# Attention feeding a feed-forward layer: the inverse sums laid out by partition in DRAM, filler products allowed earlier, and a new set of plan shifts

## The chip, the cores and the metric

The kernel runs on one core of one Trainium2 chip. The metric is device time in microseconds (us). Three runs of the kernel before gave 2834.0, 2835.68 and 2836.08 us, a median of 2835.68 us.

## What is computed

The reference is an attention over pooled keys, followed by a feed-forward layer on its result:

```
kv_flat = mean over 4x4 windows of kv, reshaped to [4, 768, 128] @ w_sr
s = q @ kv_flat^T / sqrt(128);  s -= max(s);  a = exp(s);  a /= a.sum() + 1e-9
x = a @ kv_flat                          # 4 batches x 12288 tokens x 128
h = x @ w_in;  g = h - tanh(h);  out = g @ w_out        # w_in 128 x 2048, w_out 2048 x 128
```

The weights are given in double precision and the inputs in single precision. The kernel forms the products in half precision with a high and a low part of each operand. For small `h` it computes `h - tanh(h)` from `h * tanh(c h)^2`.

## The kernel before, in words

**Tiling.** 49152 tokens are cut into 96 groups of 512, 24 to a batch. A group has four tiles of 128 tokens. For each tile PE (TensorE) makes scores against the 768 keys (L737, six products of 384 columns, tile `s`). DVE (VectorE) takes the maximum (`nm`, L745), ACT (ScalarE) the exponential and its row sum (`e`, L751) and a half precision copy (`a`, L756), and POOL (GpSimd) the low part (L760). The DMA queue of SP then transposes `a` into `at` (L764), one transpose for a tile, so that keys lie on the partitions. When four tiles of a group are there, 18 products of 512 columns form `x` (L814).

**The division.** The row sums of a group lie as [128 partitions, 4 tiles]. `inverse` (L778, L779) sums and inverts them into `inv`. The division (L827) needs these 512 numbers as one row, token by token, on every partition. So SP stores `inv` to a DRAM tile `sums_row` (L782) and reads it back, broadcast to all 128 partitions, as `row` (L786). Groups 0 and 1 do without DRAM: there PE makes the row with products against an identity, and ACT copies it (L796). DVE's `divide` then gives `xf`, from which `x2`, the high and the low part of the input of the feed-forward, is made.

**The feed-forward.** A group has eight units of 256 hidden columns. A unit is six products of 512 columns into `h` (L854 to L856), tanh and square on ACT (`t`, L882, L885), `gg` on DVE (L888), its high part `gh` on POOL or, for one unit of eight, on ACT, its low part `gl` on DVE (L899), and six products into `acc` (L860 to L862). There are two buffers of `h` and of `gg`, and one of `acc` and of `x`.

**Keys.** The keys of batches 1 to 3 are loaded in 12 pieces each (`kc`, 512 KB, L536) and pooled by DVE in 48 reductions of one size (`kvp`, L540), while the groups before run. The keys of batch 0 are pooled by PE at the start: it multiplies each of the 16 places of a window by `w_sr` and sums them in `s` (L551).

**What sets the order.** Everything above is first entered as steps of a `Plan` with an engine, an estimated duration and a place. `run` (L146) then schedules the list by these estimates; the tables `SHIFT` and `FIRST` move the place of every step of one kind (`FIRST` for the first 28 places), and `EARLY` moves a whole group. The order that comes out is the program order of each engine. Engines wait for each other by semaphores only. SP issues its DMAs in that order too, and a DMA that has to wait holds all behind it. While `run` schedules, it looks for pauses on PE in the first 75 us of its own estimate: where one is longer than 1 us, `busy` (L1143) puts products there that nobody reads (`spare`, L1151). Before, this begins only after the last pooling step of batch 0, which bears the name `pooled`.

Of the kernel before, what the change touches and what calls it, by code (L numbers as in the profile page):

```python
# [9 lines left out]
F32 = mybir.dt.float32  # L10
# [6 lines left out]
ALU = mybir.AluOpType  # L17
# [4 lines left out]
P = 128  # L22
# [45 lines left out]
class Plan:  # L68
# [8 lines left out]

    SHIFT = {
        "divide": 0.1, "exps": -1.11, "forth": 0.58, "fro": 3.81, "g_high": 1.19, "g_low": 0.61,
        "inverse": 0.91, "largest_score": -1.19, "largest_x": -0.1, "load_row": 1.46,  # L80
        "pool": 12.74, "q_high": 0.33, "q_low": 0.21, "result": -0.72, "scores": -0.17,
        "square": -0.48, "store": -1.33, "store_row": 2.86, "store_x": -1.51, "tanh": 0.29,
        "turn_weights": 0.78, "values": 1.09, "weight_high": 2.59, "weight_low": 0.56,
        "x_high": 1.25, "x_low": -6.78,
    }

    FIRST = {
        "add": -1.15, "copy": -0.44, "copy_row": -2.77, "diagonals": 1.67, "divide": 2.2,
        "exps": -0.64, "forth": 2.94, "fro": 5.42, "g_high": 7.15, "high": 1.2, "inverse": -0.87,
        "keys_wide": -2.2, "largest": 1.37, "largest_score": -0.82, "largest_share": 0.12,  # L90
        "largest_x": 0.26, "load_q": -1.09, "load_row": 1.54, "load_words": 1.25, "low": -1.78,
        "lower": 1.13, "pool": 13.24, "q_high": -1.56, "q_low": 1.38, "result": -1.78,
        "rows": 2.23, "scaled": -1.29, "scores": -3.23, "scores_wide": -2.15, "shares": -0.67,
        "shift": 1.11, "size": 0.26, "sizes": 3.78, "small": 3.11, "square": -0.1, "store": 0.64,
        "store_row": 4.53, "store_x": 3.1, "sum_of_rows": -0.86, "sums": 5.55, "tanh": -0.84,
        "times": -0.33, "top": -0.25, "turn_weights": 1.58, "upper": -1.52, "values": 0.12,
        "values_high": 0.24, "weight_high": 0.13, "weight_low": 1.91, "within": 0.68,
        "x_high": -1.77, "x_low": -4.87,
    }
    UNTIL = 28  # L100
    SOON_FIRST, FIRST_US = 0.111, 150.0

    EARLY = {"attention 0": 2.1, "attention 1": 6.6, "attention 2": 8.5, "attention 3": 2.2, "weights_in": 2.9, "weights_out": 18.9}
    KEEP_US = 75.0
    SOON = 0.153
    TURN = 0.19
# [39 lines left out]
    def run(self, between):  # L146


        n = len(self.ops)
# [16 lines left out]
            for k in need[i] | behind[i]:  # L166
                then[k].append(i)
        free, ready, done, begun, order, was_wide = {}, {}, [0.0] * n, [0.0] * n, [], True
        pooled = False
        for i in range(n):  # L170
            if not left[i]:
                ready.setdefault(self.ops[i][1], []).append((0.0, i))
        while any(ready.values()):
            best = None
            for e, q in ready.items():
                if q:
                    starts = []
                    for r, i in q:
                        held = free.get("port", 0.0) if self.ops[i][5] else 0.0
                        starts.append((max(free.get(e, 0.0), r, held), self.ops[i][0], i, r))  # L180
                    first = min(starts)[0]
                    soon = first + (self.SOON_FIRST if first < self.FIRST_US else self.SOON)
                    step, i, start, r = min((p, i, t, r) for t, p, i, r in starts if t <= soon)
                    if best is None or (start, step, i) < best[:3]:
                        best = start, step, i, e, r
            now, _, i, e, r = best
            ready[e].remove((r, i))
            step, _, us, _, late, port, dma, wide, dram = self.ops[i]
            if e == "PE":
                us += self.TURN if wide and not was_wide else 0.0  # L190
                was_wide = wide
                pause = now - free.get(e, 0.0)
                if pooled and pause > 1.0 and now < self.KEEP_US:
                    order.append((free[e], -round((pause - 0.6) / 0.3)))
                pooled = pooled or self.names["pooled"] == i
            free[e] = now + us
            if dma:
                landed = free.get("rows", 0.0) if dram == "read" else 0.0
                free["dma"] = max(free.get("dma", 0.0), now + us, landed) + dma
                if dram == "rows":  # L200
                    free["rows"] = now + us + late
                late += free["dma"] - (now + us)
            if port:
                free["port"] = now + us
            begun[i], done[i] = now, now + us + late
            order.append((now, i))
            for k in then[i]:
                left[k] -= 1
                if not left[k]:
                    f = self.ops[k][1]  # L210
                    r = [done[j] + (self.HOP if self.ops[j][1] != f else 0.0) for j in need[k]]
                    r = max(r + [begun[j] + 0.01 for j in behind[k]])
                    ready.setdefault(f, []).append((r, k))
# [3 lines left out]
        held, at = None, 1 + next(k for k, (_, i) in enumerate(order) if i == self.names["known"])  # L217
# [18 lines left out]
def attention_then_ffn(ctx: ExitStack, tc: tile.TileContext, q, kv, w_sr, w_in, w_out, out):  # L236
# [7 lines left out]
    V, A, PL, PE, SP = nc.vector, nc.scalar, nc.gpsimd, nc.tensor, nc.sync  # L244

    B, C, N = q.shape
    K, W = kv.shape[2], kv.shape[3]
# [5 lines left out]
    NGT = B * NG  # L253
# [35 lines left out]
    sums_all = const.tile([P, 2, TT, 2], F32, name="sums_all")  # L289
    ident = const.tile([P, P], F32, name="ident")  # L290
    xs = dram.tile([C, 2, B * N], F16, name="xs")
    sums_row = dram.tile([NGT, TT, P], F32, name="sums_row")

    plan.tile("ident", "ident", 1, lambda: None)
    def identity(step):
# [233 lines left out]
    def keys(b, s0):  # L529
# [25 lines left out]
        if b:  # L555
            gap, cut = 6, 4
            sb(kvp, "kvp", [P, K], F32, 1)
            for j in range(K // KB):
                s, key = s0 - gap * (K // KB - j), f"kc.{b}.{j}"
                sb(key, "kc", [P, KB, W], F32, 5)  # L560
                plan.op(s - 6, "SP", 0.5, partial(load, j, KB, key), (), (key,), late=2.0, dma=1.3,
                        dram="read", after=("unit", *divmod(int(s) - 8, UN)))
                for k in range(cut):
                    plan.op(s + k * gap / cut, "DVE", 0.33, partial(pool, j, KB, k, key), (key,),
                            ((kvp, (j, k)),))
        else:

            tags = [("t", 2), ("gg", 2), ("kc", 5)] * 2 + [("kc", 5)] * 3
            tags += [(("gh", 4), ("gl", 4))] * 4 + [("kc", 5)] * 3
            for n, tag in enumerate(tags):  # L570
                s = s0 - 40 + n
                if isinstance(tag[0], tuple):
                    for c, (name, bufs) in enumerate(tag):
                        key = f"kc.{b}.{n}.{c}"
                        sb(key, name, [P, KH], F32, bufs)
                        plan.op(s + c / 2, "SP", 0.45, partial(load_places, n, c, key), (), (key,),
                                late=2.0, dma=0.5)
                        plan.op(s + c / 2, "PE", 0.72, partial(product_of_place, n, (c,), (key,)),
                                (key,), ((pk, c),), wide=True)
                else:  # L580
                    key = f"kc.{b}.{n}"
                    sb(key, tag[0], [P, K], F32, tag[1])
                    plan.op(s, "SP", 0.45, partial(load_places, n, None, key), (), (key,), late=2.0,
                            dma=1.0)
                    plan.op(s, "PE", 1.44, partial(product_of_place, n, (0, 1), (key, key)), (key,),
                            (pk,), name="pooled" if n == W - 1 else None, wide=True)

        sb(vs, "vs", [P, 2], F32, 2)
        sb(vt, "vt", [P, 2, K], F16, 2)
# [94 lines left out]
    def attention(g, s0):  # L684
# [94 lines left out]
            V.reciprocal(out=plan[inv], in_=plan[inv])  # L779

        def store_row():
            SP.dma_start(out=sums_row[g].rearrange("t p -> p t"), in_=plan[inv])  # L782

        def load_row():
            r = sums_row[g : g + 1].rearrange("g t p -> g (t p)")
            SP.dma_start(out=plan[row], in_=r.to_broadcast([P, G]))  # L786


        def sum_of_rows():
            for t in range(TT):  # L790
                by = plan[inv][:, t : t + 1].to_broadcast([P, P])
                PE.matmul(out=plan[f"row_at.{g}"][:, t * P : (t + 1) * P], lhsT=by, rhs=ident,
                          start=True, stop=True)

        def copy_row():
            A.copy(out=plan[row], in_=plan[f"row_at.{g}"])  # L796

        s1 = s0 + 2 * TT
        plan.op(s1, "DVE", 0.25, inverse, (sums, "ident"), (inv,), late=0.1)
# [2 lines left out]
            plan.op(s1, "PE", 1.3, sum_of_rows, (inv, "ident"), (row_at,), late=0.2, wide=True)  # L802
            plan.op(s1, "ACT", 0.51, copy_row, (row_at,), (row,), late=0.1)
        else:
            plan.op(s1, "SP", 0.5, store_row, (inv,), (f"dram.{g}",), late=10.0, dma=0.8,
                    dram="rows")
            plan.op(s1, "SP", 0.5, load_row, (f"dram.{g}",), (row,), late=3.2, dma=0.65,
                    dram="read")
# [15 lines left out]
        plan.tile(f"most_x.{g}", f"most_x.{g}", 1, lambda: None)  # L824

        def divide():
            V.scalar_tensor_tensor(out=plan[xf], in0=plan[x], scalar=plan[vs][:, 0:1],  # L827
                                   in1=plan[row], op0=ALU.mult, op1=ALU.mult)

        def x_high():  # L830
            A.copy(out=plan[x2][:, 0], in_=plan[xf])
# [178 lines left out]
    def attention_any(b):  # L1010
# [31 lines left out]
        with tc.For_i(0, N, G) as place:  # L1042
# [18 lines left out]
                SP.dma_start(out=at[:, :, tok], in_=a.rearrange("p a k -> p (a k)"), transpose=True)  # L1061
            V.tensor_scalar(out=inv, in0=inv, scalar1=1e-9 * 2.0**LIFT, scalar2=None, op0=ALU.add)
            V.reciprocal(out=inv, in_=inv)
            SP.dma_start(out=sums_row[0].rearrange("t p -> p t"), in_=inv)
            row = t("row", [P, G])
            r = sums_row[0:1].rearrange("g t p -> g (t p)")
            SP.dma_start(out=row, in_=r.to_broadcast([P, G]))
            x = ps.tile([P, G], F32, tag="x", name="x_any", bufs=1)
            for n in range(KT):
                for k, (l, r) in enumerate(((n, n), (KT + n, n), (n, KT + n))):  # L1070
                    PE.matmul(out=x, lhsT=vv[:, l], rhs=at[:, r], start=(n == 0 and k == 0),
                              stop=(n == KT - 1 and k == 2))
            xf, x2 = t("xf", [P, G]), t("x2", [P, 2, G], F16, 3)
            V.scalar_tensor_tensor(out=xf, in0=x, scalar=by_batch[:, b, 6:7], in1=row,
                                   op0=ALU.mult, op1=ALU.mult)
            A.copy(out=x2[:, 0], in_=xf)
            V.tensor_tensor(out=x2[:, 1], in0=xf, in1=x2[:, 0], op=ALU.subtract)
            SP.dma_start(out=xs[:, :, bass.ds(place + b * N, G)], in_=x2)
# [129 lines left out]
```

## Time and profile before

| | |
|---|---|
| median of three runs | 2835.68 us (2834.0 to 2836.08) |
| profiled execution | 2835.5 us, span 2833.8 us |
| granted TensorE clock, mean | 0.997 |
| PE busy | 2795.2 us, 99% |
| DVE busy | 2682.0 us, 95% |
| ACT busy | 2596.9 us, 92% |
| POOL busy | 1346.5 us, 48% |

A busy share is an engine's time in instructions over the span; register, branch and DMA-issuing instructions are not counted in it. A row of the timeline gives the start, the time busy, the engine with the line and the names (out, arrow, in), and in brackets the idle time before it with what ended it. The granted clock is the share of full speed that the chip allowed TensorE.

### The profile page before, as it was taken

The page shows a single profiled execution, that of the slowest core. Times are in us where ns is not written, and L with a number is a line of the kernel's source. Part 1 is how long each engine was busy: PE and PEld are TensorE (multiplying, and loading weights), DVE is VectorE, ACT ScalarE, POOL GpSimd, SP SyncE. Part 2 cuts the span into 40 slices and gives each one's busy share as a digit, 9 for nine tenths or more (in the row PEclk, how much of TensorE's full clock was granted, in tenths as well). Part 3 has the DMA queues.
Part 4 walks back from the last instruction along what each step waited for, and adds up shares of the span by engine and source line. Part 5 has one row for each costly group of instructions (what it writes and reads, how often), then busy time and mean ns, then how long its engine had stood idle before and what let it go on. Part 6 is the DMA issues. An engine that isn't in the chain of part 4 may idle for free.

```text
span 2833.8 us, 39602 instructions
## 1 busy us (share of the span) xinstructions
PE 2795.2 (99%) x13430; PEld 1320.9 (47%) x13430; DVE 2682.0 (95%) x3201; ACT 2596.9 (92%) x3311; POOL 1346.5 (48%) x1057
## 2 busy tenths in 40 slices
PE   7999999999999999999999999999999999999998
PEld 4444444444444444444444444444444444444443
DVE  8899999999999999999999999999999999999997
ACT  7899999989999999998999999999999999999986
POOL 1455444444445454445445454444444544545442
PEclk9999999999999999999999999999999999999999
DMA  8544456555454446654544444566554444444440
GB/s 235 88 94 92 95 113 110 119 107 102 87 101 86 101 86 120 119 116 104 89 97 88 98 86 108 108 122 117 104 90 91 96 88 98 86 99 88 90 79 28
DMA packets 736421, 285.03 MB, mean 101 GB/s; under 512 B 665168, under 2 KB 692944, under 8 KB 736208
## 3 DMA queue, kind: packets, MB, share of 16 engines
q1 hardware_dynamic: 736208, 282.41, 50.0%
q8 instruction: 107, 1.75, 0.3%
q14 instruction: 106, 0.87, 0.2%
HBM read 79.23 MB, written 50.52 MB: 46 GB/s over the span
## 4 chain that ended last, share of the span: by engine, by line
PE 57%; DVE 26%; ACT 8%; issue 6%; DMA 1%; POOL 0%; DVEq 0%; SPq 0%; ACTq 0%; POOLq 0%
DVE gl L899 10%; PE s L737 8%; DVE gg L888 8%; PE x L814 7%; PE h L854 7%; PE h L856 7%; PE h L855 7%; PE acc L862 7%; PE acc L860 7%; PE acc L861 7%; DVE nm L745 4%; ACT t L882 3%; ACT e L751 2%; ACT t L885 2%; ACT a L756 1%
## 5 line engine op out<-in xcount | busy, mean ns | idle before, releaser
L892 POOL TENSOR_SCALAR gh<-gg 128x1024 f16<-128x1024 f32 x672 | 720.3, 1072 | 1231.9 <-DVE gl L899 663.4
L888 DVE SCALAR_TENSOR_TENSOR gg<-h,by_batch,t 128x1024 f32<-128x1024 f32 x768 | 983.2, 1281 | 82.3 <-ACT t L885 26.1
L899 DVE SCALAR_TENSOR_TENSOR gl<-gh,gg 128x1024 f16<-128x1024 f16 x768 | 1009.4, 1315 | 8.3 <-POOL gh L892 2.5
L882 ACT ACTIVATE t<-h,by_batch 128x1024 f32<-128x1024 f32 x768 | 849.5, 1106 | 112.8 <-PE h L856 109.2
L885 ACT ACTIVATE t<-t 128x1024 f32<-128x1024 f32 x768 | 811.3, 1056 | 21.2
L760 POOL TENSOR_TENSOR a<-e,a 128x768 f16<-128x768 f32 x380 | 625.6, 1647 | 245.8 <-ACT t L885 101.6
L854 PE MATMUL h<-x,wih 128*128 128x512 f16 x1536 | 582.0, 379 | 9.9 <-DVE gg L888 8.5
L862 PE MATMUL acc<-gl,wos 128*128 128x512 f16 x1536 | 582.6, 379 | 1.0 <-DVE gl L899 1.0
L860 PE MATMUL acc<-gh,woh 128*128 128x512 f16 x1536 | 582.7, 379 | 0.6 <-POOL gh L892 0.5
L861 PE MATMUL acc<-gh,wol 128*128 128x512 f16 x1536 | 582.6, 379 | 0.0
L855 PE MATMUL h<-x,wih 128*128 128x512 f16 x1536 | 582.0, 379 | 0.3 <-DVE x L834 0.3
L856 PE MATMUL h<-x,wil 128*128 128x512 f16 x1536 | 582.0, 379 | 0.0
L814 PE MATMUL x<-at,vv 128*128 128x512 f16 x1728 | 467.6, 380 | 5.9 <-issue 3.9
L751 ACT ACTIVATE e<-s,nm 128x768 f32<-128x768 f32 x380 | 340.0, 895 | 60.9 <-DVE nm L747 57.0
L745 DVE TENSOR_REDUCE nm<-s 128x1 f32<-128x768 f32 x380 | 361.2, 950 | 21.1 <-PE s L737 20.7
L756 ACT CAST a<-e 128x768 f16<-128x768 f32 x384 | 315.5, 822 | 2.9
L737 PE MATMUL s<-vt,qh 128*128 128x384 f16 x1520 | 309.1, 326 | 4.1 <-ACT e L751 4.1
L814 PEld LDWEIGHTS <-vv 128*128 128x128 f16 x1728 | 169.3, 98 | 210.1 <-issue 8.9
L854 PEld LDWEIGHTS <-wih 128*128 128x128 f16 x1536 | 150.0, 98 | 184.3 <-DVE gg L888 14.4
L855 PEld LDWEIGHTS <-wih 128*128 128x128 f16 x1536 | 150.0, 98 | 182.3 <-issue 20.3
L862 PEld LDWEIGHTS <-wos 128*128 128x128 f16 x1536 | 150.4, 98 | 181.5 <-issue 0.6
L856 PEld LDWEIGHTS <-wil 128*128 128x128 f16 x1536 | 150.1, 98 | 181.8 <-issue 0.6
(141 smaller groups left out, 1767.3 us busy)
## 6 DMA issues: line engine op xcount, KB each, us to landing
qs<-in_q_dram SPq DMA_DIRECT2D x96, 256.0 KB, 2.7
xs<-x SPq DMA_DIRECT2D x96, 256.0 KB, 2.4
out_dram<-o SPq DMA_DIRECT2D x96, 256.0 KB, 2.2
row<-sums_row SPq DMA_DIRECT2D x94, 256.0 KB, 4.2
kc<-in_kv_dram SPq DMA_DIRECT2D x36, 512.0 KB, 4.3
at<-a SPq DMA_TRANSPOSE x384, 4.0
kc<-in_kv_dram SPq DMA_DIRECT2D x8, 384.0 KB, 7.9
words<-in_moe_w_in_dram SPq DMA_DIRECT2D x4, 512.0 KB, 8.0
```

The source lines that it names most:

```text
L814: PE.matmul(out=plan[x], lhsT=l, rhs=r, start=(n == 0 and k == 0), stop=(n == KT - 1 and k == 2))
L854: PE.matmul(out=h, lhsT=wih[:, fs], rhs=xh, start=True, stop=False)
L855: PE.matmul(out=h, lhsT=wih[:, fs], rhs=xl, start=False, stop=False)
L856: PE.matmul(out=h, lhsT=wil[:, fs], rhs=xh, start=False, stop=True)
L860: PE.matmul(out=acc, lhsT=woh[:, fs], rhs=gh, start=(f == 0), stop=False)
L861: PE.matmul(out=acc, lhsT=wol[:, fs], rhs=gh, start=False, stop=False)
L862: PE.matmul(out=acc, lhsT=wos[:, fs], rhs=gl, start=False, stop=(f == FT - 1))
L882: A.activation(out=plan[t], in_=plan[h], func=AF.Tanh, scale=node)
L885: A.activation(out=plan[t], in_=plan[t], func=AF.Square)
L888: V.scalar_tensor_tensor(out=plan[gg], in0=plan[h], scalar=weight, in1=plan[t], op0=ALU.mult, op1=ALU.mult)
L892: return PL.tensor_scalar(out=plan[gh], in0=plan[gg], scalar1=1.0 / LOW, scalar2=1.0, op0=ALU.mult, op1=ALU.mult)
L899: return V.scalar_tensor_tensor(out=plan[gl], in0=plan[gh], scalar=-LOW, in1=plan[gg], op0=ALU.mult, op1=ALU.add)
```

## The change

Three things change.

**The layout of the inverse sums.** `sums_row` is [group, partition, tile] and no longer [group, tile, partition]. The store's 512 packets of one word become 128 packets of four words. The read stays one stretch of 2 KB for each partition, but its words come in the order partition, tile. So `divide` walks `x` and `xf` tile by tile and reads `row` with a step of four words, and `copy_row` of groups 0 and 1 writes with that step. The same edit stands in a fallback that this input does not run.

**The fillers.** The condition `pooled` is gone: pauses inside the pooling get filler products too.

**The plan.** The store's estimates fall (`late`, the time until it is there, from 10.0 to 4.5; `dma`, its share of the queue, from 0.8 to 0.5), and some numbers of the tables change: two of `SHIFT`, eight of `FIRST` and one of `EARLY`.

```diff
-        "inverse": 0.91, "largest_score": -1.19, "largest_x": -0.1, "load_row": 1.46,
-        "pool": 12.74, "q_high": 0.33, "q_low": 0.21, "result": -0.72, "scores": -0.17,
+        "inverse": 0.91, "largest_score": -1.19, "largest_x": -0.1, "load_row": 1.75,
+        "pool": 12.74, "q_high": 0.33, "q_low": 0.21, "result": -0.72, "scores": 0.17,
...
-    EARLY = {"attention 0": 2.1, "attention 1": 6.6, "attention 2": 8.5, "attention 3": 2.2, "weights_in": 2.9, "weights_out": 18.9}
+    EARLY = {"attention 0": 2.1, "attention 1": 6.6, "attention 2": 4.5, "attention 3": 2.2, "weights_in": 2.9, "weights_out": 18.9}
...
-                if pooled and pause > 1.0 and now < self.KEEP_US:
+                if free.get(e) and pause > 1.0 and now < self.KEEP_US:
                     order.append((free[e], -round((pause - 0.6) / 0.3)))
-                pooled = pooled or self.names["pooled"] == i
...
-    sums_row = dram.tile([NGT, TT, P], F32, name="sums_row")
+    sums_row = dram.tile([NGT, P, TT], F32, name="sums_row")
...
-            SP.dma_start(out=sums_row[g].rearrange("t p -> p t"), in_=plan[inv])
+            SP.dma_start(out=sums_row[g], in_=plan[inv])
...
-            r = sums_row[g : g + 1].rearrange("g t p -> g (t p)")
+            r = sums_row[g : g + 1].rearrange("g p t -> g (p t)")
             SP.dma_start(out=plan[row], in_=r.to_broadcast([P, G]))
...
+        def by_tile(ap):
+            return ap.rearrange("p (q t) -> p t q", t=TT)
...
-            A.copy(out=plan[row], in_=plan[f"row_at.{g}"])
+            at = plan[f"row_at.{g}"].rearrange("p (t q) -> p t q", t=TT)
+            A.copy(out=by_tile(plan[row]), in_=at)
...
-            plan.op(s1, "SP", 0.5, store_row, (inv,), (f"dram.{g}",), late=10.0, dma=0.8,
+            plan.op(s1, "SP", 0.5, store_row, (inv,), (f"dram.{g}",), late=4.5, dma=0.5,
                     dram="rows")
...
-            V.scalar_tensor_tensor(out=plan[xf], in0=plan[x], scalar=plan[vs][:, 0:1],
-                                   in1=plan[row], op0=ALU.mult, op1=ALU.mult)
+            to, of = (plan[k].rearrange("p (t q) -> p t q", t=TT) for k in (xf, x))
+            V.scalar_tensor_tensor(out=to, in0=of, scalar=plan[vs][:, 0:1],
+                                   in1=by_tile(plan[row]), op0=ALU.mult, op1=ALU.mult)
```

The new order of the instructions differs mostly in the groups 0 to 7. From group 8 on PE, ACT and POOL keep their order; DVE's differs in where the reductions of `kc` stand, and SP's in where the read of `row` stands.

On SP, the last transposes of groups 2 and 3 and the stores of their inverse sums. Before (`at_612` is the `at` of group 2, `at_853` that of group 3):

```order
L764 DMA_TRANSPOSE at_612<-a_685 128x12x128
L704 DMA qs_777<-in_q_dram 128x512
L782 DMA sums_row_83<-inv_806 128x4x1
L764 DMA_TRANSPOSE at_612<-a_779 128x12x128
L764 DMA_TRANSPOSE at_853<-a_809 128x12x128
L764 DMA_TRANSPOSE at_853<-a_877 128x12x128
L786 DMA row_925<-sums_row_83 128x512
L842 DMA xs_82<-x2_896 256x1x512
L764 DMA_TRANSPOSE at_853<-a_914 128x12x128
L704 DMA qs_993<-in_q_dram 128x512
L924 DMA out_dram<-o_997 128x512
L782 DMA sums_row_83<-inv_1021 128x4x1
```

And of the changed kernel (`at_617` is group 2, `at_835` group 3):

```order
L762 DMA_TRANSPOSE at_617<-a_690 128x12x128
L762 DMA_TRANSPOSE at_617<-a_771 128x12x128
L780 DMA sums_row_83<-inv_813 128x4
L762 DMA_TRANSPOSE at_835<-a_799 128x12x128
L845 DMA xs_82<-x2_831 256x1x512
L784 DMA row_892<-sums_row_83 128x512
L762 DMA_TRANSPOSE at_835<-a_873 128x12x128
L762 DMA_TRANSPOSE at_835<-a_911 128x12x128
L702 DMA qs_970<-in_q_dram 128x512
L762 DMA_TRANSPOSE at_835<-a_972 128x12x128
L927 DMA out_dram<-o_1009 128x512
L780 DMA sums_row_83<-inv_1013 128x4
```

The last transpose of group 2 (`a_779`, now `a_771`) stood behind the store and now stands ahead of it; the last of group 3 (`a_1008` before, in the row behind those shown; now `a_972`) does the same.

On PE, the end of the pooling of batch 0, with the fillers. Before:

```order
L551 MATMUL s<-gh,wsr 128x384
L551 MATMUL s<-gl,wsr 128x384
L551 MATMUL s<-kc,wsr 128x384 x6
L1151 MATMUL spare<-wsr 128x128 x12
L311 MATMUL acc<-ident,vs 128x128
```

And of the changed kernel:

```order
L549 MATMUL s<-gh,wsr 128x384
L549 MATMUL s<-gl,wsr 128x384
L549 MATMUL s<-kc,wsr 128x384 x2
L1156 MATMUL spare<-wsr 128x128 x4
L549 MATMUL s<-kc,wsr 128x384 x4
L1156 MATMUL spare<-wsr 128x128 x12
L309 MATMUL acc<-ident,vs 128x128
```

Four fillers are added before the last two places; elsewhere their number stays.

On DVE, one of the groups in which keys are pooled; the first rows follow the reciprocal of the inverse sums. Before:

```order
L540 TENSOR_REDUCE kvp<-kc 128x16 x3
L745 TENSOR_REDUCE nm<-s 128x1
L747 TENSOR_SCALAR nm<-nm 128x1
L540 TENSOR_REDUCE kvp<-kc 128x16
L899 SCALAR_TENSOR_TENSOR gl<-gh,gg 128x1024
L888 SCALAR_TENSOR_TENSOR gg<-h,by_batch,t 128x1024
L899 SCALAR_TENSOR_TENSOR gl<-gh,gg 128x1024
L888 SCALAR_TENSOR_TENSOR gg<-h,by_batch,t 128x1024
L745 TENSOR_REDUCE nm<-s 128x1
L747 TENSOR_SCALAR nm<-nm 128x1
L540 TENSOR_REDUCE kvp<-kc 128x16
L899 SCALAR_TENSOR_TENSOR gl<-gh,gg 128x1024
```

And of the changed kernel:

```order
L538 TENSOR_REDUCE kvp<-kc 128x16
L743 TENSOR_REDUCE nm<-s 128x1
L745 TENSOR_SCALAR nm<-nm 128x1
L902 SCALAR_TENSOR_TENSOR gl<-gh,gg 128x1024
L891 SCALAR_TENSOR_TENSOR gg<-h,by_batch,t 128x1024
L902 SCALAR_TENSOR_TENSOR gl<-gh,gg 128x1024
L891 SCALAR_TENSOR_TENSOR gg<-h,by_batch,t 128x1024
L743 TENSOR_REDUCE nm<-s 128x1
L745 TENSOR_SCALAR nm<-nm 128x1
L538 TENSOR_REDUCE kvp<-kc 128x16
L902 SCALAR_TENSOR_TENSOR gl<-gh,gg 128x1024
```

Here three reductions have gone from behind the reciprocal into the group before, between a `gl` and the `gg` ahead of `divide`. Three `kvp<-kc` at that place stood in 9 groups and stand in 18; a cycle of three groups held 4, 8 and 4 reductions and now holds 7, 5 and 4.

## Rows read from the trace of the kernel before

**Rows 1.** Windows: start:end, length, busy PE, PEld, DVE, ACT, POOL (counts), clock, DMA, GB/s

```profile
50.00:150.00 100.00, 90.75 (x445) 43.84 (x445) 86.78 (x119) 88.59 (x128) 46.12 (x35) 0.97 0.62 110
2000.00:2500.00 500.00, 498.88 (x2408) 235.41 (x2407) 476.30 (x551) 466.80 (x596) 246.82 (x192) 1.00 0.47 93
```

**Rows 2.** Timeline of PE around the two longest pauses of its steady work

```profile
95.72 1.44 PE L814 MATMUL x<-at,vv 128*128 128x512 f16 x3 [3.86 <-issue]
...
99.52 2.48 PE L814 MATMUL x<-at,vv 128*128 128x512 f16 x6
101.84 0.81 PE L737 MATMUL s<-vt,qh 128*128 128x384 f16 x4
...
120.48 0.81 PE L814 MATMUL x<-at,vv 128*128 128x512 f16 x3 [1.96 <-DVE gl L899]
121.13 0.38 PE L854 MATMUL h<-x,wih 128*128 128x512 f16 x1
```

**Rows 3.** Window behind the first of these pauses

```profile
96.00:98.00 2.00, 2.00 (x6) 0.76 (x5) 2.00 (x2) 0.00 (x0) 0.80 (x1) 0.50 1.02 217
```

**Rows 4.** Timeline of SP, 84 to 92 us

```profile
85.63 4.23 SPq L764 DMA_TRANSPOSE at<-a  x2
```

**Rows 5.** DMAs issued from 85.5 to 88 us: size, median us to landing

```profile
at<-a SPq DMA_TRANSPOSE x1, 10.0
```

**Rows 6.** DMAs issued from 111.5 to 115 us

```profile
at<-a SPq DMA_TRANSPOSE x1, 6.9
```

**Rows 7.** DMAs issued in the whole run

```profile
out_dram<-o SPq DMA_DIRECT2D x96, 256.0 KB, 2.2
...
kc<-in_kv_dram SPq DMA_DIRECT2D x36, 512.0 KB, 4.3
at<-a SPq DMA_TRANSPOSE x384, 4.0
...
sums_row<-inv SPq DMA_DIRECT2D x94, 2.0 KB, 9.0
```

**Rows 8.** Timeline of PE in the pooling of batch 0

```profile
15.38 2.85 PE L551 MATMUL s<-kc,wsr 128*128 128x384 f32 x8 [0.24 <-DMA kc<-in_kv_dram]
...
29.09 4.78 PE L551 MATMUL s<-kc,wsr 128*128 128x384 f32 x8 [2.55 <-DMA kc<-in_kv_dram]
33.70 2.84 PE L1151 MATMUL spare<-wsr 128*128 128x128 f32 x24
```

**Rows 9.** Timeline of DVE behind that pooling

```profile
33.90 0.96 DVE L606 TENSOR_REDUCE vs<-s 128x1 f32<-128x768 f32 x1 [0.37 <-PE s L551]
```

**Rows 10.** Timeline of DVE at one of the 9 places

```profile
433.68 1.06 DVE L540 TENSOR_REDUCE kvp<-kc 128x16 f32<-128x256 f32 x3
```

**Rows 11.** Timeline of PE behind it

```profile
439.27 0.38 PE L862 MATMUL acc<-gl,wos 128*128 128x512 f16 x1
440.04 0.39 PE L854 MATMUL h<-x,wih 128*128 128x512 f16 x1 [0.38 <-DVE gg L888]
```

**Rows 12.** Groups of DVE by shape: busy, mean ns of one, idle before

```profile
L888 DVE SCALAR_TENSOR_TENSOR gg<-h,by_batch,t 128x1024 f32<-128x1024 f32 x768 | 983.2, 1281 | 82.3 <-ACT t L885 26.1 <-ACT a L756 1.0 <-DVE gl L899 0.9
...
L827 DVE SCALAR_TENSOR_TENSOR xf<-x,vs,row 128x512 f32<-128x512 f32 x96 | 71.3, 742 | 0.0
...
L365 DVE SCALAR_TENSOR_TENSOR at<-words,ym 128x512 int32<-128x512 int32 x4 | 2.8, 693 | 0.1
```

**Rows 13.** Timeline of DVE behind a division

```profile
2311.48 1.28 DVE L888 SCALAR_TENSOR_TENSOR gg<-h,by_batch,t 128x1024 f32<-128x1024 f32 x1
```

**Rows 14.** Timeline of PE at the product that this `gg` frees

```profile
2313.05 0.38 PE L854 MATMUL h<-x,wih 128*128 128x512 f16 x1
```

**Rows 15.** Timeline of SP at a load of keys

```profile
479.19 0.40 SPq L782 DMA_DIRECT2D sums_row<-inv  x1
...
481.75 1.03 SPq L536 DMA_DIRECT2D kc<-in_kv_dram  x1
489.98 0.33 SPq L786 DMA_DIRECT2D row<-sums_row  x1
```

More of the change, by code (lines that the diff above doesn't have):

```diff
@@ L87 @@
     FIRST = {
-        "add": -1.15, "copy": -0.44, "copy_row": -2.77, "diagonals": 1.67, "divide": 2.2,
-        "exps": -0.64, "forth": 2.94, "fro": 5.42, "g_high": 7.15, "high": 1.2, "inverse": -0.87,
+        "add": -1.15, "copy": -0.42, "copy_row": -2.77, "diagonals": 1.67, "divide": 2.2,
+        "exps": -0.48, "forth": 2.94, "fro": 5.36, "g_high": 5.63, "high": 1.2, "inverse": -0.87,
         "keys_wide": -2.2, "largest": 1.37, "largest_score": -0.82, "largest_share": 0.12,
@@ L93 @@
         "rows": 2.23, "scaled": -1.29, "scores": -3.23, "scores_wide": -2.15, "shares": -0.67,
[L94 to L98, printed above, removed]
+        "shift": 1.11, "size": -0.12, "sizes": 3.78, "small": 3.11, "square": -0.1,
+        "store": 0.64, "store_row": 4.53, "store_x": 3.1, "sum_of_rows": -0.86, "sums": 5.55,
+        "tanh": 0.69, "times": -0.33, "top": -0.25, "turn_weights": 3.06, "upper": -1.52,
+        "values": 0.12, "values_high": 0.24, "weight_high": 0.13, "weight_low": 1.91,
+        "within": 0.68, "x_high": -1.77, "x_low": -4.63,
     }
@@ L168, in run @@
         free, ready, done, begun, order, was_wide = {}, {}, [0.0] * n, [0.0] * n, [], True
-        pooled = False
         for i in range(n):
@@ L585, in keys @@
                     plan.op(s, "PE", 1.44, partial(product_of_place, n, (0, 1), (key, key)), (key,),
-                            (pk,), name="pooled" if n == W - 1 else None, wide=True)
+                            (pk,), wide=True)
         sb(vs, "vs", [P, 2], F32, 2)
@@ L1063, in attention_any @@
             V.reciprocal(out=inv, in_=inv)
-            SP.dma_start(out=sums_row[0].rearrange("t p -> p t"), in_=inv)
+            SP.dma_start(out=sums_row[0], in_=inv)
             row = t("row", [P, G])
-            r = sums_row[0:1].rearrange("g t p -> g (t p)")
+            r = sums_row[0:1].rearrange("g p t -> g (p t)")
             SP.dma_start(out=row, in_=r.to_broadcast([P, G]))
@@ L1073, in attention_any @@
             xf, x2 = t("xf", [P, G]), t("x2", [P, 2, G], F16, 3)
-            V.scalar_tensor_tensor(out=xf, in0=x, scalar=by_batch[:, b, 6:7], in1=row,
-                                   op0=ALU.mult, op1=ALU.mult)
+            to, of = (ap.rearrange("p (t q) -> p t q", t=TT) for ap in (xf, x))
+            V.scalar_tensor_tensor(out=to, in0=of, scalar=by_batch[:, b, 6:7],
+                                   in1=row.rearrange("p (q t) -> p t q", t=TT), op0=ALU.mult,
+                                   op1=ALU.mult)
             A.copy(out=x2[:, 0], in_=xf)
```

## The prediction, on record before the changed kernel was run

> **What bounds the kernel now.** I read the windows first. In the steady part PE is busy 498.88 of 500 us at full clock, and DVE 476.30 [rows 1]. PE is the bound there, and a change that leaves its products alone can gain next to nothing; 96 groups in that state make up most of the span. From 50 to 150 us PE is busy only 90.75 of 100 us at a clock of 0.97, so time is to be had there. The timeline of PE shows where it sits: one pause of 3.86 us before 95.72, and one of 1.96 before 120.48, both ahead of the first products of an `x` (groups 2 and 3) [rows 2]. The page names other releasers for them ("issue", a `gl`), but these products read `at`, whose last transpose comes late. SP issued that of group 2 at 85.63, next in the queue behind the store of the inverse sums [rows 4]; it landed 10.0 us later [rows 5], at about 95.6, when the product starts. That of group 3, behind its group's store too, landed 6.9 after its issue [rows 6]. A transpose takes 4.0 in the median [rows 7]. So the late transpose behind the store is the cause of both pauses. [...]
>
> **The change part by part.** All against the profiled execution, 2835.5 us with a span of 2833.8; it lies 0.2 below the median of 2835.68.
>
> *Group 2's pause.* In the new order the last transpose of group 2 is issued ahead of the store, and the store has a quarter of the packets. If the pause goes, 3.86 us go. The clock's share: from 95.72 to 101.84 PE does 15 products of 512 columns (three, six and six) in 6.12 us; three of them take 121.13 − 120.48 = 0.65 at full clock [rows 2], so 15 take 3.25, and 2.87 are lost. Together −6.7. Late next are DVE and ACT: from 50 to 150 us they are busy 86.78 and 88.59 [rows 1], and in a stretch shorter by 8.7 that is 95% and 97%, against 95% and 93% in the steady part (476.30 and 466.80 of 500). They just fit, hence a reserve below. Bounds: −6.7 to 0.
>
> *Group 3's pause.* The same move: −2.0, from 0 to −2.0. There is no lower clock to win back; right behind it products take 0.65 for three.
>
> *Fillers in the pooling.* They stand in a pause of 2.55 us before the last two places. Eight products behind it took 4.78, against 2.85 for the same eight earlier [rows 8]: 1.9 us of lower clock. The fillers take 2.84 / 24 × 8 = 0.95 (each shows as two), inside the 2.55. Even if the clock then stays up, DVE's next step on the pooled sums waited for PE only 0.37 [rows 9]; before that DVE was busy unpacking weights. I take −0.3, from −0.4 to 0; late next is that unpacking.
>
> *Reductions of the keys.* Three of them take 1.06 us [rows 10]; at the place where DVE has the least slack PE then waits: a step of 0.77 between two products that otherwise stand 0.22 apart [rows 11], so 0.55. This place now occurs 18 times in place of 9. If the trio alone decides, that is 9 × 0.55 = +5.0. If the number of reductions in the group decides, groups with 8 become groups with 7 and 5 and lose one or three reductions of 0.35 ahead of the place: 0.55 − 0.35 = 0.2 in one and none in the other, 9 × (0.2 − 0.55) = −3.2. The trio that goes gives DVE 1.06 us back behind the reciprocal, in the same cycle of three groups, so I lean to the second and take +1.0, with both ends kept.
>
> *The division.* It now reads `row` at a step of 16 bytes. Its 742 ns are those of other products of 512 elements [rows 12]. The nearest rows that bound a step: one that reads `words` at a step of 8 bytes takes 693, no more [rows 12]; twice the elements in a row take 1281. I take 0 by the first, and up to 1281 − 742 = 0.54 for each by the second; the other way 742 − 693 = 0.05 could be won on each, which nothing waits for. What hides a longer division: the `gg` after it ends at 2311.48 + 1.28 = 2312.76 [rows 13], and the product it frees starts at 2313.05 [rows 14], 0.29 later. So up to 0.29 costs nothing, and 0.54 costs 0.25 for each of 96, +24. [...] The two copies of ACT that write at this step, groups 0 and 1, go with it: 0, to at most +0.5 each.
>
> *The store itself.* 512 packets landed after 9.0 in the median, a plain store of 128 packets and 256 KB after 2.2 [rows 7]. A quarter of the excess leaves 2.2 + 6.8 / 4 = 3.9, from 2.2 to 9.0. In the steady part nothing of PE waits for it, so it is worth 0 there. [...]
>
> *Other moves* of the groups 0 to 7, with DVE and ACT nearly full: +1.0, from 0 to +4.
>
> Sum: −6.7 − 2.0 − 0.3 + 1.0 + 0 + 0 + 1.0 = −7.0, so 2828.5 for an execution like the profiled one, and 2828.7 as a median. About 0.2%, 5.7 us, is what a measurement of this kernel can tell from no change: faster means below 2830.0, slower above 2841.4.
>
> **The rivals.**
>
> *B, the division gets slower.* 96 divisions longer by 0.54 less the slack of 0.29 cost +24; with the gain of 7.0, 2852.7. It becomes slower than before in sum from 0.29 + 7.0 / 96 = 0.36 a division on. For it: `row` is read one word in 16 bytes, which nothing in this trace does. Against it: the step of 8 bytes costs nothing. [...]
>
> *C, the keys come late.* SP issues the read of `row` ahead of a load of keys; before it came after (keys at 481.75, the read at 489.98, when the store of 479.19 had landed) [rows 15]. If 16-byte packets land no sooner, the keys wait behind it, are issued at about 490.3 and land 4.3 later [rows 7], at 494.6. A moved trio would stand at about 490.9: 433.68 [rows 10] and two groups of 28.6, each 114 products of 0.217 and 24 at three quarters of that. So DVE stands 3.7 us; less 0.3 of slack, 9 × 3.4 = +31 against the −7: 2859. It decides from a landing of some 7.4 us on. For it: the trace shows 10 us for such stores. Against it: the packets are fewer by four.
>
> *D, the pauses come back elsewhere.* DVE and ACT fill 95 and 97% of the shortened stretch, so one of them may hold PE at another place of 50 to 150 us; if two thirds of 8.7 return, 2834.5. For it: ACT would be above its steady 93%. Against it: the pauses hang on one transpose, and PE's wait ends when it lands.
>
> *E, the trio costs in full.* +5.0 in place of +1.0: 2832.7.
>
> **How the numbers follow.** My forecast has 58%: its own range is 2823 to 2833, by −3.2 or +5 for the keys and 0 to +4 for the rest, and 53 of the 58 lie below 2830.0. D has 14% (2 faster, 12 same), E 10%, all within 0.2%. B has 13% and C 5%, all slower. So faster 0.55, same 0.27, slower 0.18. From 2821 to 2842 lie the forecast, D and E, and a small part of B; what is left out is the rest of B and C, 16%, and some 3% below.
>
> **What would show each step.** No pause of over 1 us before the `x` of groups 2 and 3, a clock of 1.0 from 96 to 102 us, and the two transposes landing in 4 to 5 us confirm the first two terms. The pooling's last eight products at 2.85 and a wait of DVE for `s` at zero show the fillers. The division's mean against 742 decides B. The wait of `h` for `gg` in groups with pooled keys, twice in three groups or fewer, decides E; a wait of DVE for `kc`, and stores landing above 7, show C. The prediction is wrong if the division's mean rises by more than 0.3 us, or if PE is busy below 96 of 100 us between 50 and 150 with a new releaser.

## The result and the profile after

The changed kernel took 2846.41 us (median of 6 runs, 2846.02 to 2846.52) against 2835.88 for the kernel before on the same chip (2834.0 to 2838.01): 0.38% slower, ratio 1.0038, 95% interval 1.0028 to 1.0048. I had predicted 2828.7, with 2821 to 2842 and 18% for slower. The time is rival B's in kind, and it lies outside the range.

The first term came as forecast. These are the windows of the changed kernel that answer to [rows 1, 3]:

```profile
50.00:150.00 100.00, 94.72 (x476) 46.16 (x475) 94.13 (x128) 95.98 (x135) 51.37 (x36) 1.00 0.62 120
2000.00:2500.00 500.00, 497.92 (x2394) 232.82 (x2393) 474.07 (x549) 463.12 (x592) 248.99 (x190) 1.00 0.44 95
96.00:98.00 2.00, 2.00 (x12) 0.96 (x10) 1.86 (x4) 1.97 (x3) 1.92 (x2) 1.00 0.86 148
```

From 50 to 150 us PE does 476 products where it did 445, at full clock. Yet in the steady stretch it does 2394 where it did 2408, and is busy 0.96 us less of 500. The timeline of PE has no idle time any more ahead of the products of `x` of groups 2 and 3; the first ones of group 2 answer to [rows 2]:

```profile
93.12 0.81 PE L816 MATMUL x<-at,vv 128*128 128x512 f16 x3
95.06 0.81 PE L816 MATMUL x<-at,vv 128*128 128x512 f16 x3
```

The loss stands in one line of DVE's groups by shape, the division, against 742 ns in [rows 12]; the other products keep their durations:

```profile
L891 DVE SCALAR_TENSOR_TENSOR gg<-h,by_batch,t 128x1024 f32<-128x1024 f32 x768 | 983.0, 1280 | 97.3 <-ACT t L888 47.8 <-DVE gl L902 0.5 <-ACT e L749 0.5
...
L830 DVE SCALAR_TENSOR_TENSOR xf<-x,vs,row 128x512 f32<-128x512 f32 x96 | 110.5, 1151 | 0.0
```

That is 0.41 us more on each of 96. The waits of PE (us in total, times, longest) show who pays: the weight loads, which run beside products, and the products of `h`, for the `gg` that follows the division on DVE. First the changed kernel, then the kernel before:

```profile
PEld L857 <- DVE gg L891: 55.3, 97, 1.3
...
PE h L857 <- DVE gg L891: 14.4, 27, 1.3
```

```profile
PEld L854 <- DVE gg L888: 14.4, 23, 0.9
PE h L854 <- DVE gg L888: 8.5, 25, 1.3
```

How much of the 0.41 is paid depends on the group. In a steady group the timeline of DVE, and then of PE, show the `gg` behind the division end at 2321.81 + 1.27 = 2323.08 and the freed product start at 2323.14, 0.29 behind the product at 2322.85, where that one stands 0.22 behind the product before it:

```profile
2318.57 1.14 DVE L830 SCALAR_TENSOR_TENSOR xf<-x,vs,row 128x512 f32<-128x512 f32 x1
...
2321.81 1.27 DVE L891 SCALAR_TENSOR_TENSOR gg<-h,by_batch,t 128x1024 f32<-128x1024 f32 x1
```

```profile
2322.85 0.38 PE L865 MATMUL acc<-gl,wos 128*128 128x512 f16 x1
2323.14 0.39 PE L857 MATMUL h<-x,wih 128*128 128x512 f16 x1
```

So 0.07 is lost there, and 0.34 was hidden (I had read a slack of 0.29). Where a trio of key reductions ahead of the division is the last of seven reductions since the division before (it closes a group of seven), nothing is hidden. Timeline of DVE, then of PE, at such a place:

```profile
399.87 1.06 DVE L538 TENSOR_REDUCE kvp<-kc 128x16 f32<-128x256 f32 x3
400.85 1.27 DVE L891 SCALAR_TENSOR_TENSOR gg<-h,by_batch,t 128x1024 f32<-128x1024 f32 x1
402.04 1.18 DVE L830 SCALAR_TENSOR_TENSOR xf<-x,vs,row 128x512 f32<-128x512 f32 x1
```

```profile
406.66 0.39 PE L857 MATMUL h<-x,wih 128*128 128x512 f16 x1 [0.82 <-DVE gg L891]
```

PE stood idle 0.38 at such a place before, where the trio closed a group of eight [rows 11], and stands 0.82 now.

The step stands in one more place. The two copies of ACT that write `row` for groups 0 and 1 take 1062 ns, against 562 before. ACT's groups by shape of the changed kernel, then of the kernel before:

```profile
L798 ACT COPY row<-x 128x512 f32<-128x512 f32 x2 | 2.1, 1062 | 0.0
```

```profile
L796 ACT COPY row<-x 128x512 f32<-128x512 f32 x2 | 1.1, 562 | 0.0
```

### The profile page after: what moved, and what is told of

Read it like the earlier page. It is cut to its first block, busy times and chain, and to the rows that moved or that the text cites. A ratio compares the mean times of both kernels' runs of the same rounds, so it can differ in the third digit from the quotient of the medians.

```text
span 2844.7 us, 39617 instructions
## 1 busy us (share of the span) xinstructions
PE 2802.1 (99%) x13438; PEld 1314.2 (46%) x13438; DVE 2692.0 (95%) x3201; ACT 2594.7 (91%) x3311; POOL 1382.3 (49%) x1057
## 4 chain that ended last, share of the span: by engine, by line
PE 55%; DVE 25%; ACT 8%; issue 6%; POOL 0%; DMA 0%; DVEq 0%; ACTq 0%; POOLq 0%
DVE gl L902 9%; DVE gg L891 8%; PE s L735 7%; PE x L816 7%; PE h L857 7%; PE h L859 7%; PE h L858 7%; PE acc L865 7%; PE acc L863 7%; PE acc L864 7%; DVE nm L743 4%; ACT t L885 3%; ACT a L754 2%; DVE xf L830 2%; DVE kvp L538 1%
## 5 line engine op out<-in xcount | busy, mean ns | idle before, releaser
L895 POOL TENSOR_SCALAR gh<-gg 128x1024 f16<-128x1024 f32 x672 | 755.9, 1125 | 1209.6 <-DVE gl L902 613.0
L902 DVE SCALAR_TENSOR_TENSOR gl<-gh,gg 128x1024 f16<-128x1024 f16 x768 | 981.5, 1278 | 11.2 <-POOL gh L895 5.4
L857 PE MATMUL h<-x,wih 128*128 128x512 f16 x1536 | 582.7, 379 | 17.3 <-DVE gg L891 14.4
L857 PEld LDWEIGHTS <-wih 128*128 128x128 f16 x1536 | 149.9, 98 | 216.2 <-DVE gg L891 55.3
L863 PEld LDWEIGHTS <-woh 128*128 128x128 f16 x1536 | 150.4, 98 | 173.0 <-issue 1.5
```

What stands on the lines that cost most here:

```text
L857: PE.matmul(out=h, lhsT=wih[:, fs], rhs=xh, start=True, stop=False)
L863: PE.matmul(out=acc, lhsT=woh[:, fs], rhs=gh, start=(f == 0), stop=False)
L895: return PL.tensor_scalar(out=plan[gh], in0=plan[gg], scalar1=1.0 / LOW, scalar2=1.0, op0=ALU.mult, op1=ALU.mult)
L902: return V.scalar_tensor_tensor(out=plan[gl], in0=plan[gh], scalar=-LOW, in1=plan[gg], op0=ALU.mult, op1=ALU.add)
```

## The experiments

All were timed in five rounds or more against the kernel before on the same chip, 2837.66 us (first four) and 2837.42 (last four), except the one with eight ways of reading, which had one run.

**The old layout with the new plan.** The order of every engine is that of the changed kernel.

```diff
-    sums_row = dram.tile([NGT, P, TT], F32, name="sums_row")
+    sums_row = dram.tile([NGT, TT, P], F32, name="sums_row")
...
-            SP.dma_start(out=sums_row[g], in_=plan[inv])
+            SP.dma_start(out=sums_row[g].rearrange("t p -> p t"), in_=plan[inv])
```

with the read of `row` and the division as they were before.

> The changed kernel with the inverse sums laid out as before (512 packets of one word, a plain read in the division); plan, estimates and fillers as changed, and the order of every engine that of the changed kernel. Theory S (the division's read at a step of 16 bytes is the loss; it costs 0.41 us a division, of which groups without keys hide 0.33 and groups with keys little): the 16 us that PE waits more from 150 us on go, and the gain of 7 at the start stays: 2829 to 2831. Rival K (the moved trios of key reductions cost by themselves what the groups with keys lost, 8 us): 2837 to 2840. Rival C (a store of 9 us now stands ahead of the loads of keys): 2840 or more, with DVE waiting for keys.

Measured: 2855.73 us, ratio 1.0068 (1.0055 to 1.0082). Neither S nor K; this is C. The timeline of SP of this kernel shows the read of `row` standing for the store and the load of keys behind it:

```profile
476.60 0.40 SPq L780 DMA_DIRECT2D sums_row<-inv  x1
...
487.30 0.33 SPq L784 DMA_DIRECT2D row<-sums_row  x1
487.69 0.42 SPq L534 DMA_DIRECT2D kc<-in_kv_dram  x1
```

and its timelines of DVE and of PE show the price:

```profile
492.79 1.07 DVE L538 TENSOR_REDUCE kvp<-kc 128x16 f32<-128x256 f32 x3 [3.68 <-DMA kc<-in_kv_dram]
```

```profile
495.11 0.38 PE L855 MATMUL h<-x,wih 128*128 128x512 f16 x1 [2.70 <-DVE gg L889]
```

Its waits sum this up:

```profile
PE h L855 <- DVE gg L889: 33.2, 30, 2.8
DVE kvp L538 <- DMA kc<-in_kv_dram: 27.1, 9, 3.8
```

The store of 476.60 landed 10.7 us after its issue, and the read of `row` was issued then. So the new plan needs the quick store; in the changed kernel the same load of keys is issued 3.65 us behind the store and no such wait exists.

**The new layout with the old plan.** The same lines in the kernel before, the other way round.

> The kernel before with the new layout of the inverse sums alone (128 packets, a read at a step of 16 bytes); plan, estimates and fillers as before. Theory S: 60 groups without keys lose 0.08 us each and those at the start of a batch some more, 7.6 in all, and the 27 groups with keys 0.08 to 0.41 each, 2 to 11: 2845 to 2854. Rival K: only the 7.6, so 2842 to 2844, and the old place of the trio costs no more than the 0.74 us that it did. If the store behind which the transpose stands is the cause of the early pauses, these two shorten here too, since the store is quicker: 3 to 7 us less than said.

Measured: 2850.82 us, ratio 1.0046 (1.0032 to 1.0060), 13.2 above the kernel before: S. From 50 to 150 us PE is busy 95.73 here, as the window shows, though the old order still puts the two transposes behind the store:

```profile
50.00:150.00 100.00, 95.73 (x483) 47.18 (x483) 95.93 (x129) 96.79 (x137) 48.74 (x36) 1.00 0.59 120
```

These two transposes, issued at 87.92 and 109.11, landed after 3.7 and 3.6 us, against 10.0 and 6.9 in [rows 5, 6]. In the whole run 83 transposes are issued right behind a store; they landed after 3.7 in the median here and after 9.3 in the kernel before, in the same order.

So the quick store, 2.1 us in the median here, takes the pauses away by itself, and the new order was not needed for them. The new order takes them away by itself too: in the run with the old layout the timeline of PE has no idle time ahead of the `x` of groups 2 and 3 either. A new pause stands there between the products of `x` of group 2, whose cause I did not follow:

```profile
107.56 1.10 PE L735 MATMUL s<-vt,qh 128*128 128x384 f16 x4 [2.26 <-ACT e L749]
```

**The changed kernel with a plain read of the row.** Each token gets another token's inverse sum.

```diff
-                                   in1=by_tile(plan[row]), op0=ALU.mult, op1=ALU.mult)
+                                   in1=plan[row].rearrange("p (t q) -> p t q", t=TT),
+                                   op0=ALU.mult, op1=ALU.mult)
```

> The changed kernel, but the division reads the row of inverse sums without a step, so that each token gets another token's inverse; all else as changed. Theory S: the division takes 0.74 us again, and the time is that of the old layout with the new plan or up to 1 us less: 2828 to 2831. Rival K: 2837 to 2840. Rival C tells the two layouts apart: this one has the quick store and would be 5 to 20 us below the run with the old layout.

Measured: 2823.48 us, ratio 0.9952 (0.9938 to 0.9965), lower than either theory had it. This run gains 14.2 us on its kernel before, and the changed kernel loses 10.5 on its own; the one operand's step is the difference. By the spans of the two profiled executions it is 2844.7 − 2821.7 = 23.0. PE's waits for `gg` are close to those of the kernel before, 14.4 and 8.5 us there:

```profile
PEld L858 <- DVE gg L892: 17.8, 35, 0.9
...
PE h L858 <- DVE gg L892: 8.8, 24, 1.3
```

Twice as many trios, and hardly more wait: K falls. Behind each of the nine trios that close a group of seven PE loses 0.55, as behind the nine of the kernel before [rows 11]; behind the nine that close a group of five it loses nothing. Timeline of DVE, then of PE, at one of the first nine:

```profile
396.87 1.06 DVE L538 TENSOR_REDUCE kvp<-kc 128x16 f32<-128x256 f32 x3
```

```profile
403.22 0.39 PE L858 MATMUL h<-x,wih 128*128 128x512 f16 x1 [0.38 <-DVE gg L892]
```

What PE loses can be summed from the starts of its products: the time from each start to the next, less what stands between the starts of products in an unbroken row at a clock of 1.00 (0.2158 us for 512 columns, 0.1625 for 384, in the mean of the changed kernel's trace). So summed, the 27 groups with pooled keys lost 9.6 us in the kernel before, 7.0 here, and 18.2 in the changed kernel. The step thus costs 0.41 in each of these groups, its full price, and 0.16 in each of the other 60 from group 8 on (17.1 less 7.7).

**Eight ways of reading in turn**, by the group's number.

```diff
+            if way in ("two", "four", "eight", "sixteen"):
+                t = steps[way]
+                to, of, by = tiles(to, t), tiles(of, t), words(by, t)
+            if way in ("both", "from_psum", "into"):
+                across = lambda ap: ap.rearrange("p (t q) -> p q t", t=TT)
+                flat = lambda ap: ap.rearrange("p (q t) -> p q t", t=TT)
+                to = flat(to) if way == "from_psum" else across(to)
+                of = flat(of) if way == "into" else across(of)
+                by = flat(by)
```

> The changed kernel, in which the division of groups 8 to 95 takes turns among eight ways of reading: the row at a step of 2, 4, 8 and 16 words; no step at all; the product x in PSUM read across its four tiles (a step of 128 words) with a plain row; the same step on the write alone; and on both. Only the way with 4 words and the one with both divide by the right sums. [...] Rival (the price grows with the step): 2 words some 0.8, 8 words above 1.15 and 16 above that. For the steps of 128 words there is no row yet: 0.74 to 1.2 from PSUM or on the write; where both together cost 0.74, the layout can be had without the loss.

DVE's groups by shape of this kernel, the name telling the way:

```profile
L844 DVE SCALAR_TENSOR_TENSOR xf_four<-x,vs,row 128x512 f32<-128x512 f32 x19 | 22.0, 1159 | 0.0
...
L844 DVE SCALAR_TENSOR_TENSOR xf_eight<-x,vs,row 128x512 f32<-128x512 f32 x11 | 12.5, 1132 | 0.0
L844 DVE SCALAR_TENSOR_TENSOR xf_both<-x,vs,row 128x512 f32<-128x512 f32 x11 | 12.3, 1117 | 0.0
L844 DVE SCALAR_TENSOR_TENSOR xf_into<-x,vs,row 128x512 f32<-128x512 f32 x11 | 12.3, 1115 | 0.0
L844 DVE SCALAR_TENSOR_TENSOR xf_sixteen<-x,vs,row 128x512 f32<-128x512 f32 x11 | 11.9, 1084 | 0.0
L844 DVE SCALAR_TENSOR_TENSOR xf_from_psum<-x,vs,row 128x512 f32<-128x512 f32 x11 | 8.2, 742 | 0.0
L844 DVE SCALAR_TENSOR_TENSOR xf_two<-x,vs,row 128x512 f32<-128x512 f32 x11 | 8.2, 742 | 0.0
L844 DVE SCALAR_TENSOR_TENSOR xf_plain<-x,vs,row 128x512 f32<-128x512 f32 x11 | 8.1, 741 | 0.0
```

Two words cost nothing; four cost 0.42, and more words no more than that. The price has an edge between 8 and 16 bytes and does not grow with the step from there on, up to 64 bytes. A step of 512 bytes costs 0.37 on a write to SBUF and nothing on a read from PSUM. One run, 2836.91 us in all.

**Every fourth token to a tile.** The step goes to where it was free.

```diff
-                        PE.matmul(out=plan[s][:, c * G : c * G + KH], lhsT=plan[l][:, tok],
+                        PE.matmul(out=plan[s][:, c * G : c * G + KH], lhsT=plan[l].rearrange("p (q t) -> p t q", t=TT)[:, t],
...
+            to, by = (plan[k].rearrange("p (q t) -> p q t", t=TT) for k in (xf, row))
+            V.scalar_tensor_tensor(out=to, in0=plan[x].rearrange("p (t q) -> p q t", t=TT),
+                                   scalar=plan[vs][:, 0:1], in1=by, op0=ALU.mult, op1=ALU.mult)
```

> The changed kernel with the step moved to where the run with eight ways showed it free: a tile of 128 tokens now takes every fourth token of the group (PE loads the weights of the scores at a step of four half words), so the row of inverse sums comes in the order of the tokens; the division reads the row plainly, reads x in PSUM across its four tiles and writes plainly. Theory S (the step on SBUF costs, that on PSUM does not): the division takes 0.74 us and the time is that of the changed kernel with a plain read, 2823 to 2825. Rival W (weights loaded at a step of 8 bytes take longer, and PE waits for them): each group loads 24 of them; where one takes 0.1 us more and none of it is hidden, 96 x 24 x 0.1 = 230 us, so 2830 to 3050, and the weight loads' mean, 98 ns before, shows it.

Measured: 2823.88 us, ratio 0.9953 (0.9939 to 0.9966), with a division of 741 ns: S. W shows in the weight loads, 98 ns before, but they lie beside products, and the time is within 0.4 us of the run with the plain read:

```profile
L735 PEld LDWEIGHTS <-qh 128*128 128x128 f16 x1536 | 174.0, 113 | 126.7 <-issue 6.1
```

**The old condition for the fillers.** The condition `pooled` in `run` as before; only the four fillers differ in the order.

> The changed kernel without the four fillers inside the pooling (the condition of the kernel before is back); the rest of every engine's order as changed. My forecast's term: 0.3 us slower than the changed kernel, since DVE is late there in any case: 2846.4 to 2847. Rival F (the clock that stays up is worth more, as PE waits 1.7 us less before the first division in the changed kernel): 2848 to 2849, with a granted clock of 0.5 to 0.7 from 30 to 34 us and the last eight pooling products at 4.8 us instead of 2.9.

Measured: 2847.17 us (2846.12 to 2847.68), 0.8 above the changed kernel, between the two forecasts; the ratios, each to its own runs of the kernel before, 1.0035 (1.0022 to 1.0047) and 1.0038 (1.0028 to 1.0048), do not tell them apart. In the windows of this kernel and of the changed one the lower clock is there and gone:

```profile
30.00:34.00 4.00, 4.00 (x10) 2.11 (x10) 3.25 (x6) 3.49 (x7) 0.00 (x0) 0.66 0.54 198
```

```profile
30.00:34.00 4.00, 3.27 (x15) 1.92 (x14) 3.29 (x6) 3.42 (x7) 0.00 (x0) 1.00 0.52 187
```

It is worth little, since DVE comes to the pooled sums at 34.02 in the changed kernel, at 33.90 before [rows 9].

**Packets of two words.** The sums of a group are stored in 256 packets of 8 bytes, and the row is read at a step of two words.

```diff
-    sums_row = dram.tile([NGT, P, TT], F32, name="sums_row")
+    sums_row = dram.tile([NGT, 2, P, 2], F32, name="sums_row")
...
-            return ap.rearrange("p (q t) -> p t q", t=TT)
+            return ap.rearrange("p (q l) -> p l q", l=2)
```

> The changed kernel with the inverse sums stored in 256 packets of two words, and a division that reads the row at a step of two words, 8 bytes (the tiles of a group are paired, so that the step stays one); order of every engine as changed. [...] If the store's landing goes by its packets, 2.1 at 128 and 8.7 at 512 give 4.3 at 256, the keys are in time (they were late at 8.7, and my sum put the limit at 7.4), and the time is 2823 to 2826. Rival (a packet of 8 bytes costs as one of 4, and the landing stays at 7 or more): DVE waits for keys again, 2830 to 2850.

Measured: 2823.29 us, ratio 0.9951 (0.9937 to 0.9964), the division 742 ns, as two words took in the run with eight ways. The store landed after 3.2, below the 4.3 by packets; DVE waits for no keys. The copies of ACT, at the same step, take 600 ns. The rows of DMAs of this kernel and of the changed one, against 9.0 in [rows 7]:

```profile
sums_row<-inv SPq DMA_DIRECT2D x94, 2.0 KB, 3.2
```

```profile
sums_row<-inv SPq DMA_DIRECT2D x94, 2.0 KB, 2.1
```

**The old layout and the old estimates for the store, with the new tables.**

```diff
-            plan.op(s1, "SP", 0.5, store_row, (inv,), (f"dram.{g}",), late=4.5, dma=0.5,
+            plan.op(s1, "SP", 0.5, store_row, (inv,), (f"dram.{g}",), late=10.0, dma=0.8,
```

> The old layout with the new tables and fillers, as in the first run, but with the planner's old estimates for the store (10.0 and 0.8): the loads of keys then stand ahead of the read of the row in SP's order again. The order of the first groups differs from both kernels. Theory C (the 27 us that DVE waited for keys, and the 33 that PE waited for DVE, in the first run come from that place in the queue): the wait for keys is gone, below 2 us, and the time is 2824 to 2838, by how the first groups come out. Rival (the keys are late for the number of trios or for the slow store's load on the queue): DVE still waits 10 us or more for keys, and the time stays above 2845.

Measured: 2841.83 us, ratio 1.0014 (1.0005 to 1.0023). No wait of DVE for keys is left in its trace, as C has it. This run does not tell C from the number of trios, though: the old estimates moved the reductions too, and trios ahead of the `gg` before a division stand in 6 places where the run with the old layout has 18. What tells them apart is the run with the plain read: its order is that of the run with the old layout, 18 trios included, its store is quick, 2.1 us in the median, and DVE waits for no keys.

The time is 3.8 above what I gave. From 150 to 1000 us PE loses 20.7 here (6.8 in the kernel before), summed as above; ahead of that it loses 8.8 less than the kernel before, and behind it the two are level. The order of the groups in that stretch differs from both kernels; I did not follow it further.

## Why the prediction was wrong

- **The pauses of groups 2 and 3**, −6.7 and −2.0: right. Summed as above, the run with the plain read loses 6.2 and 2.0 less between the divisions that enclose these two places, and PE's busy time from 50 to 150 us rose by 4 to 5 us of 100, the clock from 0.97 to 1.00. The 94.72 of the changed kernel lie below the 96 that I had set as a sign of being wrong; what is left are mostly waits for `e` ahead of the scores at 53.44 and 58.71, 1.33 and 1.06, which were 0.97 and 1.06 before, and the division's price. My first reason, the transpose moved ahead of the store, was not needed: the quicker store alone does it, as the new order alone does. The two transposes behind the store waited for it: in the kernel before they landed 1.1 and 0.2 us after it.
- **The division**, 0 taken, 0 to +24 kept: the step that failed. I chose the end of the nearest row, a step of 8 bytes that costs nothing. That row could not speak for 16 bytes. The runs show 0.41 for each, 23 us in all; with eight ways in one run it was 742 ns at two words, as against 741 plain, and 1159 at four. They show where the price begins, not what in DVE or SBUF makes it. The price of rival B, 24, was right to 1 us, but by luck, since it is built from two errors that cancel: 0.54 was more than 0.41, and the slack of 0.29 does not exist in the groups with pooled keys. The copies of ACT, 0 to +0.5 each, came out at the upper end, 0.50 longer.
- **The reductions of the keys**, +1.0: the sign was wrong, the size small. Without the step these groups lose 2.6 less than before. Neither the trio nor the count decides alone: a trio that closes seven reductions costs 0.55, where I had 0.2, and one that closes five costs nothing, as I had said. So E did not come. The gain lies mostly in small waits inside the groups of four, 3.5 us in 18 of them before and 1.4 in 9 in the run with the plain read.
- **The fillers**, −0.3: not distinguishable from 0 by time; the clock from 30 to 34 us was 0.66 without the four and 1.00 with them, as said.
- **The store**, 3.9 taken, 2.2 to 9.0: measured 2.1, the plain store's end. My estimate of a quarter of the excess was too dear.
- **Rival C**: not in the changed kernel, but in the run with the old layout, and near the sizes that I gave. I had a stand of 3.7 for DVE in 9 places; it was 3.68 at the place shown, and 3.0 in the mean of 9. I had +31; the run with the plain read, of the same order, is 32.3 quicker.
- **The sum without the division** was −7.0; the run with the plain read gives −14.2 against its own kernel before, and −12.1 by the spans. Summed as above, 7.5 of it lies in the groups 0 to 7, 1.9 ahead of the first division and 2.6 in the keys. The two pauses gave 8.2 and the groups 0 to 7 together only 7.5, so some 0.7 of my reserve of +1.0 for a full DVE and ACT was needed: group 0 loses 1.1 more than before. In the run with packets of two words it does not, which points to ACT's longer copy and not to rival D.

The chance of 13% for B was too low: against it stood only a row at a step of 8 bytes, which did not test 16.

## What to carry to other kernels

When a DMA's packets are made larger by another layout, look at what then reads the layout: a step of 16 to 64 bytes on DVE's operand in SBUF cost 0.34 to 0.42 us for 512 words, while a step of 8 bytes there and a step of 512 bytes on a read from PSUM cost nothing (742 ns each, 741 with no step). The two versions that have only such steps in the division beat both kernels, at 2823.3 and 2823.9 us. And where no row tests an operation at its own step, keep the dear end of the estimate at a real chance rather than take the nearest row that costs nothing.

## What I had not expected of the hardware

A step of 16 words (64 bytes) was cheaper than one of 4, 1084 against 1159 ns, with 11 and 19 instructions. Weight loads at a step of 8 bytes took 113 ns for 98. A store of 128 packets landed after 2.1 us, one of 256 after 3.2 and one of 512 after 8.7 to 9.3, so the landing does not go in line with the packets; whether their number or their size decides, no run tells. A transpose right behind the store of 512 packets landed with it, after 9.3 in the median where others took 3.9. ACT's copy of 512 words, writing at a step of 16 bytes, took 1062 ns, at 8 bytes 600 and plainly 562, two copies each.
